# A fused attention and expert kernel on one core: a rotating fourth PSUM bank, no idle matmuls in the first steps, one more unit transposed by the crossbar, the last rows in three parts

## Chip, cores, metric

One core of a Trainium2 chip. The metric is the device time of one execution in microseconds (us). A program on one core has no other cores beside it to compare, so the state of a run is judged by its distance from the fastest run of the same kernel.

Differences in this study are tenths of a microsecond of some 475. For these the medians are too coarse. I therefore also use a second measure: the same ScalarE and VectorE instructions are paired in two traces, and the difference of their start times, from the start of each span, is read along the execution. It is called the **shift** below; negative is earlier than in the kernel before. Where no view of the profile shows a thing, it was read from the packed trace itself.

## The reference, cut

Attention over 4 batches, 8 heads, 768 rows of 64; queries and keys are assigned to one of 16 clusters, and only equal clusters see each other. The result, 3072 rows of 512, goes through four experts, weighted row by row.

```python
q_assign = argmax(q_n @ c_n.T); k_assign = argmax(k_n @ c_n.T)      # 16 clusters per head
mask = q_assign[:, :, :, None] == k_assign[:, :, None, :]
attn = softmax(where(mask, scale * q @ k.T, -1e9)); x = (attn @ v)   # -> 3072 x 512
p = domain_probs / (domain_probs.sum(-1, keepdims=True) + 1e-09)
for e in range(4):
    out += p[:, e:e + 1] * (maximum(x @ w1[e], 0) @ w2[e])           # 512 -> 1024 -> 512
```

## The kernel before

The mask is folded into the score product: 64 rows of a head's queries and keys are followed by 16 one-hot rows. Attention runs in steps of 512 scores, and the experts of earlier rows are woven between the steps so that TensorE always has work. A *unit* is 128 or 256 rows of the attention result.

PSUM has eight banks. Four of them matter here: three tagged `mo` and one tagged `misc`.

```python
PS_BUFS = {"s": 2, "av": 1, "av2": 1, "mo": 3, "misc": 1}
# ...
    ph = bank("mo")                    # expert, first layer:  eight matmuls of 256 columns
    po = bank("mo")[:, c]              # expert, second layer: eight matmuls of up to 512 columns
# ... scores of the cluster assignment of the next batch:
    put(at, lambda x=x, t=("mo", "misc")[z]: x.scores_split(t))
```

In the first steps an idle matmul stands ahead of the score matmuls. It writes zeros that the scores overwrite, and is there to hold TensorE's clock:

```python
WARM = range(4, 14)
# ... in attention(), one per step:
    if now in WARM:
        nc.tensor.matmul(sp[:, :256], blank[:, :128], blank[:, :256], start=True, stop=True)
    for x, (h, y) in enumerate(blocks[z:z + per] if b < ROWS else ()):
        nc.tensor.matmul(sp[:, x * n:(x + 1) * n], KF[...], QF[...], start=True, stop=True)
```

The one-hot rows of the keys of heads 6 and 7 come from other partitions, by four small transfers from SyncE's queue (`keep` copies to `oht`, `send` moves 16 x 384 elements of bf16, 12 KB):

```python
7: lambda: (k1.onehot(2), puts(k1, 0), k1.keep(), k1.send_all((2, 3))),
8: lambda: (qb.onehot_narrow(), qb.put_narrow(slice(0, 2), "dve")),
9: lambda: (puts(k1, 1), qb.put_narrow(slice(2, HG), "dve")),
```

The attention result is turned for the experts, by TensorE and a VectorE copy for the first four units, by the DMA crossbar for the rest:

```python
    if us[0] > 3:
        for m in range(nr):
            nc.sync.dma_start(out=xTs[us[0]][:, h2 // 2, m * 128:(m + 1) * 128],
                              in_=xn[:, m].rearrange("p j d -> p (j d)"), transpose=True)
        return
    due.setdefault(now + D_T + (us[0] > 1), []).append(turn)   # two TensorE transposes and dve()
```

The last 128 rows of the last expert are closed in two parts, so that the end is short:

```python
    end = (u, e, m) == (NU - 1, E - 1, len(rs) - 1)
    for c in (slice(0, DM // 2), slice(DM // 2, DM)) if end else (slice(0, DM),):
        po = bank("mo")[:, c]
        # eight matmuls, then oacc = po * p + oacc on VectorE
        if e == E - 1:
            nc.sync.dma_start(out=out[...], in_=oacc[:, c])
```

The softmax here doesn't subtract the row's maximum and nothing guards it: scores larger than these inputs give would overflow.

## Time and profile before

| | median | runs |
|---|---|---|
| time before | 476.23 us | 475.79 to 476.75 (4; the first three alone have the median 476.54) |
| span of the profiled execution | 473.6 us | |
| TensorE, busy share of the span | 98% | |
| all idle time of TensorE that the list of waits shows | 3.3 us in nine lines | |

In lines of a profile, PE is TensorE's matmuls, PEld its weight loads, DVE VectorE, ACT ScalarE, POOL GpSimd, and SPq the queue of transfers that SyncE issues; L728 is line 728 of the kernel. A row for a stretch of time gives its length, the busy us and the count of instructions of PE, PEld, DVE, ACT and POOL, then the granted clock, the busy share of the DMA engines and GB/s.

From the page of the kernel before: the span, and the two costliest groups of TensorE (source line, engine, operation, output and inputs, count; busy us, mean ns; idle time ahead of them):

```profile
span 473.6 us, 11333 instructions
...
L728 PE MATMUL ps_mo<-xT,w1b 128*128 128x256 bf16 (+1 forms) x1664 | 195.7, 264 | 0.0
...
L747 PE MATMUL ps_mo<-w2b,hT 128*128 128x512 bf16 (+1 forms) x725 | 186.2, 377 | 2.3
```

These are the two layers of the experts, in `mo` banks alone.

### The profile page before, as it was taken

Reading aid. Unit: us, or ns where it says so; the run is one execution under the profiler, and the core shown is the slowest. Engines: PE = TensorE matmul, PEld = TensorE weight load, DVE = VectorE, ACT = ScalarE, POOL = GpSimd, SP = SyncE. Lnnn points to the kernel's source line nnn. Section 1 sums busy time; section 2 is a strip of 40 time slices with the busy share of each in tenths; the row PEclk is TensorE's granted clock in tenths of the full one; section 3 lists DMA queues with packets and bytes.
Section 4 is the critical chain, followed back from the end, with each engine's and each line's share of the span. In section 5 each row is a group of like instructions: output and inputs, shape, how many; then the busy total and the mean of one; then the engine's idle time right before and its main releaser. Section 6 shows DMA issues by size and latency. Waiting matters only on the chain.

```text
span 473.6 us, 11333 instructions
## 1 busy us (share of the span) xinstructions
PE 464.2 (98%) x4488; PEld 333.2 (70%) x4539; DVE 227.1 (48%) x561; ACT 277.1 (59%) x502; POOL 187.8 (40%) x301
## 2 busy tenths in 40 slices
PE   8999999999999999999999999999999999999997
PEld 5778777777776767677676767776766766767665
DVE  5964764322315654322234544423878757665112
ACT  5767655454665556566555655665665685664342
POOL 5936469283353776370443942000332132221000
PEclk9999999999999999999999999999999999999999
DMA  8999962925564842603565657202100100100101
GB/s 279 259 211 345 240 123 35 173 44 164 98 126 108 197 104 41 154 21 60 154 141 122 118 113 160 68 20 70 51 12 8 53 11 8 35 29 12 44 2 45
DMA packets 74557, 48.01 MB, mean 101 GB/s; under 512 B 50248, under 2 KB 69256, under 8 KB 74504
## 3 DMA queue, kind: packets, MB, share of 16 engines
q1 hardware_dynamic: 65256, 37.96, 32.0%
q0 software_dynamic: 8576, 9.25, 11.0%
q8 instruction: 35, 0.57, 0.5%
q10 hardware_dynamic: 672, 0.08, 0.1%
q14 instruction: 18, 0.15, 0.1%
HBM read 37.31 MB, written 6.30 MB: 92 GB/s over the span
## 4 chain that ended last, share of the span: by engine, by line
PE 96%; DVE 1%; issue 1%; ACT 1%; ACTq 0%
PE ps_mo L728 35%; PE ps_mo L747 34%; PE ps_s L638 10%; PE ps_av L665 8%; PE ps_s L548 1%; PE ps_mo L242 1%; PE ps_misc L242 1%; PE ps_misc L548 1%; PE ps_s L87 1%; PE ps_mo L267 1%; PE ps_mo L400 1%; PE ps_misc L267 1%; PE ps_misc L400 1%; DVE oh L287 0%; DVE mx L284 0%
## 5 line engine op out<-in xcount | busy, mean ns | idle before, releaser
L644 ACT ACTIVATE at<-ps_s 128x512 bf16<-128x512 f32 x252 | 147.7, 595 | 118.3 <-PE ps_s L638 102.9
L728 PE MATMUL ps_mo<-xT,w1b 128*128 128x256 bf16 (+1 forms) x1664 | 195.7, 264 | 0.0
L747 PE MATMUL ps_mo<-w2b,hT 128*128 128x512 bf16 (+1 forms) x725 | 186.2, 377 | 2.3
L728 PEld LDWEIGHTS <-w1b 128*128 128x128 bf16 x1664 | 146.3, 98 | 25.0 <-issue 1.2
L734 ACT ACTIVATE hT<-ps_mo 128x512 bf16<-128x512 f32 x192 | 114.8, 598 | 60.9 <-PE ps_mo L728 58.0
L756 DVE SCALAR_TENSOR_TENSOR oacc<-ps_mo,psb,oacc 128x512 f32<-128x512 f32 (+1 forms) x73 | 54.1, 742 | 127.0 <-PE ps_mo L747 122.5
L747 PEld LDWEIGHTS <-hT 128*128 128x128 bf16 x776 | 67.0, 98 | 57.5 <-issue 3.1
L638 PE MATMUL ps_s<-qf,kf 80*128 80x256 bf16 (+1 forms) x456 | 82.8, 267 | 0.5 <-DMA kf<-oht 0.2
L665 PEld LDWEIGHTS <-at 128*128 128x128 bf16 x1152 | 69.9, 97 | 15.3 <-issue 1.7
L665 PE MATMUL ps_av<-vx,at 128*128 128x65 bf16 x1152 | 80.3, 193 | 0.2
L651 POOL TENSOR_TENSOR at<-at,same 128x512 bf16<-128x512 bf16 x24 | 28.3, 1177 | 96.6 <-ACT at L644 81.1
L638 PEld LDWEIGHTS <-kf 80*128 80x128 bf16 x456 | 42.5, 98 | 20.2 <-issue 1.3
L565 DVE TENSOR_SCALAR same<-qf,late 128x256 bf16<-128x256 bf16 x144 | 39.1, 324 | 0.0
L377 POOL COPY t<-t 128x768 uint16<-128x768 uint16 x32 | 36.3, 1143 | 0.0
L651 DVE TENSOR_TENSOR at<-at,same 128x512 bf16<-128x512 bf16 x48 | 21.6, 451 | 25.9 <-ACT at L644 25.8
L358 POOL COPY h<-raw 128x768 uint16<-128x768 uint16 x16 | 13.1, 829 | 36.0 <-DMA raw<-in_q_dram 29.7
L672 DVE RECIPROCAL zr<-ps_av 128x4 f32<-128x4 f32 (+1 forms) x50 | 8.9, 179 | 34.2 <-PE ps_av L665 34.1
L336 POOL DMA_DIRECT2D kf<-oht x32 | 15.5, 494 | 24.5 <-DMA oht<-oh 15.1
L361 POOL COPY h<-raw 128x768 uint16<-128x768 uint16 x16 | 13.5, 857 | 28.8 <-DMA raw<-in_q_dram 16.9
L754 DVE TENSOR_SCALAR oacc<-ps_mo,psb 128x512 f32<-128x512 f32 x18 | 13.5, 747 | 23.4 <-PE ps_mo L747 23.3
L416 POOL COPY st<-sct 128x384 uint16<-128x384 uint16 x16 | 10.7, 713 | 31.4 <-DMA sct<-scs 20.7
L336 POOL DMA_DIRECT2D qf<-oht x40 | 20.1, 510 | 4.5 <-DVE oht L313 3.9
(132 smaller groups left out, 288.4 us busy)
## 6 DMA issues: line engine op xcount, KB each, us to landing
raw<-in_v_dram SPq DMA_DIRECT2D x8, 768.0 KB, 6.6
out_dram<-oacc SPq DMA_DIRECT2D x23, 256.0 KB, 2.0
raw<-in_k_dram SPq DMA_DIRECT2D x7, 768.0 KB, 6.3
raw<-in_q_dram SPq DMA_DIRECT2D x6, 768.0 KB, 5.0
w1b<-in_moe_w_dram POOLq DMA_DIRECT2D x4, 1024.0 KB, 11.4
w2b<-in_moe_w_dram POOLq DMA_DIRECT2D x4, 1024.0 KB, 16.8
qf<-nos SPq DMA_DIRECT2D x2, 768.0 KB, 4.4
xT<-xn SPq DMA_TRANSPOSE x72, 2.4
```

The lines of the kernel that those rows point to most:

```text
L336: (nc.gpsimd if self.b or self.i0 and self.g else nc.sync).dma_start(out=self.rows(slice(D, D + CL), j, r), in_=self.oht[p0:p0 + CL, :self.w])
L361: pool(self.h16[:, z * HG * QW + c:z * HG * QW + c + 2 * QW], self.halves(raw[self.b, self.t, self.g])[:, 2 * c:2 * c + 4 * QW][:, z::2])
L377: pool(self.all[:, y * w:(y + 1) * w].bitcast(U16)[:, z::2], self.t16[:, (2 * z + y) * w:(2 * z + y + 1) * w])
L565: nc.vector.tensor_scalar(same[:, x * 256:(x + 1) * 256], clusters(b)[:, g, w, k // 2, k % 2, :], key_nos[b % 2][:, g, 8 * i + 4 * (k // 2 ...
L638: nc.tensor.matmul(sp[:, x * n:(x + 1) * n], KF[b % 2][:K, h, r, i * 128:(i + 1) * 128], QF[b % 2][:K, h, rs[0]:rs[-1] + 1, w * 128:(w + 1 ...
L644: nc.scalar.activation(at, sp, ACT.Exp, scale=scale)
L651: (nc.gpsimd if n4 in POOL_STEPS else nc.vector).tensor_tensor(at, at, same_cluster(b, w, cur), op=ALU.mult)
L665: nc.tensor.matmul(av[:, h % 2, m, :], at[:, c0:c0 + 128], VX[b % 2][:, h, 2 * i + r, :], start=(first and x == 0 and m == 0), stop=(last ...
L728: nc.tensor.matmul(ph[:, x * n:(x + 1) * n], W1[e][:, i, (f + x) * 128:(f + x + 1) * 128], xT[:, i, :], start=(i == 0), stop=(i == ND - 1))
L734: nc.scalar.activation(ht, ph, ACT.Relu)
L747: nc.tensor.matmul(po, hT[f // per][:, c0:c0 + 128], W2[e][:, f, c], start=(f == 0), stop=(f == NF - 1))
L756: nc.vector.scalar_tensor_tensor(oacc[:, c], po, pap, oacc[:, c], op0=ALU.mult, op1=ALU.add)
```

## The change

The intent: a fourth bank, free in the middle batches, joins the three that the experts use. The idle matmuls, which cost TensorE time, go. The fourth unit's eight transposes leave TensorE for the crossbar. The last rows close in three parts, the last half as long as before.

```diff
+    spare, turns = False, 0
+    def ring():
+        nonlocal turns
+        turns += 1
+        return bank("misc" if spare and turns % 4 == 0 else "mo")
@@ assignment scores
-            put(at, lambda x=x, t=("mo", "misc")[z]: x.scores_split(t))
+            put(at, x.scores_split)                  # takes ring() inside
@@ attention
-    WARM = range(4, 14)
-                    if now in WARM:
-                        nc.tensor.matmul(sp[:, :256], blank[:, :128], blank[:, :256],
-                                         start=True, stop=True)
-                            if us[0] > 3:
+                            if us[0] > 2:
@@ expert
-            ph = bank("mo")
+            ph = ring()
-            for c in (slice(0, DM // 2), slice(DM // 2, DM)) if end else (slice(0, DM),):
-                po = bank("mo")[:, c]
+            for c in (slice(0, 256), slice(256, 384), slice(384, DM)) if end else (slice(0, DM),):
+                po = ring()[:, c]
@@ woven
+                spare = PER_B + 4 <= step < PER_B * (B - 1)
```

More of the change, by code (lines that the diff above doesn't have):

```diff
@@ L390, in casts, with scores_split @@
             dve(late(self.t, self.b)[:, y:y + HG // 2], self.rows_of())
-        def scores_split(self, bank_tag):
-            sc = bank(bank_tag)
+        def scores_split(self):
+            sc = ring()
             for x in range(HG):
@@ L900, in woven @@
     def woven(works, upto):
+        nonlocal spare
         base, spent = step, 0.0
```

## The prediction

> **What bounds the kernel now.** I read the busy shares and the slices first, then the list of waits for TensorE alone, then busy time by stretches, then the groups, and last the timelines of the two ends.
>
> From the page of the kernel before (engines: busy us, share of the span, instructions; then tenths in 40 slices of 11.8 us):
>
> ```profile
> PE 464.2 (98%) x4488; PEld 333.2 (70%) x4539; DVE 227.1 (48%) x561; ACT 277.1 (59%) x502; POOL 187.8 (40%) x301
> PE   8999999999999999999999999999999999999997
> PEclk9999999999999999999999999999999999999999
> PE 96%; DVE 1%; issue 1%; ACT 1%; ACTq 0%
> ```
>
> TensorE is the bound from end to end: 98% busy, 96% of the chain that ended last. No other engine is over 59%. A busy share alone does not show that nothing is left, so I asked for waits. All idle time of TensorE over the span, by what ended it (us in total, times, longest):
>
> ```profile
> PE ps_s L87 <- DVE blank L80: 1.2, 1, 1.2
> PE ps_mo L276 <- ACT scs L271: 0.4, 1, 0.4
> PE ps_misc L296 <- DVE oh L287: 0.4, 2, 0.2
> PE ps_mo L296 <- DVE oh L287: 0.3, 1, 0.3
> PE ps_mo L267 <- DVE bdc L187: 0.2, 1, 0.2
> PE ps_s L638 <- DMA kf<-oht: 0.2, 1, 0.2
> PE ps_s L634 <- ACT at L644: 0.2, 1, 0.2
> ```
>
> No line has an expert matmul (L728, L747) waiting for its bank. The same query over 60 to 320 us, where the four banks will rotate, returns no wait at all. Busy time in two stretches of that part:
>
> ```profile
> 100.00:140.00 40.00, 39.74 (x385) 29.45 (x389) 11.92 (x21) 22.46 (x41) 19.22 (x45) 1.00 0.52 120
> 220.00:260.00 40.00, 39.79 (x378) 28.90 (x380) 12.40 (x24) 23.74 (x43) 14.39 (x17) 1.00 0.55 129
> ```
>
> The first pair after the length is TensorE: 39.7 of 40 us. Since ends of matmuls are modelled, I also took start-to-start distances from the trace: 109 ns for 256 columns, 216 ns for 512, 56 ns for 128, with a 90th percentile within 1 ns of the median. A distance of 432 ns occurs, but it is twice 216, and 725 of 768 second-layer matmuls are recorded, so those are lost records. Summed, what 60 to 320 us show above these distances is under 1 us, mostly around the small fp32 matmuls of L400.
>
> **What the Trainium skill says.** (1) "TensorE: Matmul & The Clock Gate", section "Wait — 56ns, not 53.3ns?": back-to-back distance is columns over 2.4 GHz plus some 2.5 ns, which gives 55.8, 109 and 216 ns. The trace agrees to 1 ns, so the middle is at the rate of the array. (2) "Perfetto Trace Analysis", its opening note: matmul busy time is a bad metric of what is left, as matmuls are pipelined. Hence the distances above. (3) The TensorE page, "What's actually happening": the clock halves after about one idle window of 3.4 us. That bears on taking idle matmuls out. The granted clock here is 1.00 in every stretch from 5.7 us on, also where the matmul stream fills only 0.65 (5.7 to 9.1) and 0.71 (9.1 to 12.5) of the time. (4) "DMA: Bandwidth & Descriptors", "Anatomy of one DMA": most of a transfer's fixed 2 us is waiting for the written bytes to be confirmed, not size. The trace agrees: the last output is issued at 470.86, its packets end at 472.3, the span at 473.6.
>
> **Part 1, four rotating banks.** Removes no instruction and adds none: the order listing has the same expert matmuls, with every fourth bank another one, and the score copies in the other bank. It can only shorten waits for banks on the path. There are none between 60 and 320 us. ScalarE and VectorE wait for TensorE there (58.0 us of ScalarE for L728, 122.5 us of VectorE for L747), so the readers of the banks are early, not late. Gain: 0.0, at most 0.2 us.
>
> **Part 2, ten idle matmuls less.** They are the group L634, ten of 256 columns between 15.6 and 22.9 us. On TensorE alone they are 10 x 0.109 = 1.09 us, and the chain of waits has them on it. But the path beside it is almost as long. SyncE and TensorE at that place:
>
> ```profile
> 19.36 2.50 SPq L336 DMA_DIRECT2D kf<-oht  x4
> ...
> 24.00 0.40 PE L638 MATMUL ps_s<-qf,kf 80*128 80x128 bf16 x4
> ...
> 26.09 0.33 PE L638 MATMUL ps_s<-qf,kf 80*128 80x128 bf16 x3 [0.18 <-DMA kf<-oht]
> ```
>
> The scores of heads 6 and 7 need four small transfers of one-hot rows. Their landings, from the semaphores in the trace, are 24.02, 24.60, 25.29 and 25.95 us, and the score matmuls that need them start at 24.23, 24.73, 25.43 and 26.09: each within 0.2 us of its landing. The transfers leave when VectorE has written their source (18.97 to 19.33), which follows a chain of transposes, maximum and comparison (16.03 to 18.31) that waits for VectorE twice. Of the ten matmuls only the first (15.58) stands ahead of that chain; two stand inside a wait for VectorE (idle 0.35 at 17.80), and the seven later ones stand beside the transfers. So of 1.09 us I expect 0.1 us to arrive: 0.11 of the first, and at most 0.2 us of slack at the landings. The rest becomes longer waits for these transfers. Clock: with the ten gone the stream still fills 0.69 of 15.9 to 19.3 and 0.75 of 19.3 to 22.7 (0.81 and 0.87 before), not below what kept full clock earlier.
>
> **Part 3, the fourth unit by the crossbar.** Group before (count, busy us, mean ns):
>
> ```profile
> L681 PE MATMUL ps_mo<-identb,xn 128*128 128x128 bf16 x24 | 3.7, 220 | 0.2 <-DVE xn L674 0.2
> ```
>
> Eight of these 24 go (71 to 111 us), with four VectorE copies. They stand in the dense part, so each is worth its distance: 8 x 0.056 = 0.45 us, all on the path. In exchange SyncE gets eight crossbar transposes of 1.2 us issue each. Is the data late then? Of the last head pair, VectorE is done at 105.7. SyncE's order puts it behind three transposes that end at 106.96; two issues more and 2.4 us to landing make about 110.5. The unit's first matmul (L728) starts at 117.73. Seven us of room: nothing comes back.
>
> **Part 4, the last rows in three parts.** The end of the kernel before:
>
> ```profile
> 470.16 1.03 SPq L759 DMA_DIRECT2D out_dram<-oacc  x2
> 470.35 0.48 DVE L756 SCALAR_TENSOR_TENSOR oacc<-ps_mo,psb,oacc 128x256 f32<-128x256 f32 x1 [0.39 <-PE ps_mo L747]
> ```
>
> TensorE: 8 x 0.109 = 0.87 becomes 16 x 0.056 = 0.89 us, +0.02. VectorE's last piece: 512 columns take 0.745 and 256 take 0.480 (both rows in the trace), so 1.035 ns a column and 128 fewer columns save 0.13 us. The piece before takes 0.35 us and ends before the last matmul (0.45 us later). The last transfer halves to 64 KB: of its 2.7 us only the packets' part shrinks (estimate 0.05 to 0.1 us, from 8 packets per engine at 46 ns). Sum: -0.2 us.
>
> **Sum.** 0.0 - 0.1 - 0.45 - 0.2 = -0.75 us: 476.54 becomes 475.8 us.
>
> **The rivals.** (a) All ten idle matmuls count, because the transfers land earlier than now once they are issued earlier. Then -1.09 in place of -0.1: 474.8. For it: L634 is on the chain. Against: the landings decide 24.2 to 26.1, and the queues are full there (DMA share over 1.0 in every stretch from 3 to 33 us). (b) Removed idle matmuls cost the clock: one or two windows of 3.4 us at half rate, so +2 to +4 us: 478 to 480. Against: the shares above. I give it 4%. (c) The rotation does pay, through bank waits that the records hide: a few ns at each of some 190 evictions, 0.5 to 1 us. Against: the median distances equal the array's rate. (d) The crossbar transposes hold up SyncE's in-order queue, and input loads behind them (109 us) start 2.4 us later. GpSimd waits for those loads, but their results are used 25 us later: no change expected.
>
> **Range and chances.** The runs of the kernel before span 1.0 us (475.79 to 476.75), as large as the effect. Half of (a) gives 475.3; everything failing but part 3 gives 476.1. With the scatter of a median (about 0.4 us) I take 474.9 to 476.6. A change over 2% means 9.5 us. Nothing here reaches that: all idle time of TensorE listed above is under 3 us. So within 2% has 0.99.
>
> **What will show it.** Part 1: TensorE's idle list over 60 to 320 us is empty in both, and the busy time by stretches is equal. Part 2: L634 gone, granted clock still 1.00, and the idle time of TensorE (or of its weight loads, which the profile calls issue) between 15 and 27 us up by about 1 us, with the first unit's expert matmuls (28.8 us before) starting only 0.1 us earlier. If they start a full us earlier, rival (a) is right. Part 3: L681 x16, and the distance between a point at 65 and one at 120 us shorter by 0.45 us. Part 4: from the last matmul to the end of the span 0.2 us less. I am wrong by more than the range if the clock falls after 15 us, or if middle stretches shorten by more than 0.5 us beyond part 3.

## The result

Ratios here are the mean time of one kernel's fast runs over that of the other's of the same rounds, so they are not quite the ratio of the medians quoted beside them.

| | before | after |
|---|---|---|
| median (runs) | 476.23 (475.79 to 476.75, 4) | 475.87 (475.32 to 476.10, 4) |
| profiled span | 473.60 | 473.54 |

The ratio is 0.999, 95% interval 0.9973 to 1.0008: **the same**. The prediction said 475.8 in a range of 474.9 to 476.6. The page of the kernel after, same parts as shown of the kernel before:

```profile
span 473.5 us, 11380 instructions
...
PE 466.0 (98%) x4529; PEld 332.2 (70%) x4529; DVE 226.9 (48%) x558; ACT 277.2 (59%) x502; POOL 187.5 (40%) x301
...
PEclk9999999999999999999999999999999999999999
...
PE 95%; DVE 2%; DMA 1%; issue 0%; ACT 0%; SPq 0%; ACTq 0%
```

TensorE went up in busy time (464.2 to 466.0) with less work. That is no slowdown: x4529 equals the weight loads' x4529, while before 4488 of 4539 were recorded. No record of a matmul is lost this time. The clock row is full throughout.

The list of waits of TensorE over the whole span (us in total, times, longest; the first six of eight lines):

```profile
PE ps_s L95 <- DVE blank L88: 1.2, 1, 1.2
PE ps_misc L304 <- DVE oh L295: 0.6, 2, 0.4
PE ps_s L642 <- ACT at L648: 0.4, 2, 0.3
PE ps_mo L284 <- ACT scs L279: 0.4, 1, 0.4
PE ps_mo L304 <- DVE oh L295: 0.4, 1, 0.4
PE ps_s L642 <- DMA kf<-oht: 0.4, 2, 0.2
```

Line numbers are 4 to 8 higher than before at these places. All of these lie at the start. Three have grown most: the wait for `oh` in `misc` (0.4 to 0.6), for ScalarE's `at` (0.2 to 0.4) and for the transfers `kf<-oht` (0.2 to 0.4). Between 60 and 320 us the list is empty, as it was. The same two stretches of the middle (TensorE's busy us first):

```profile
100.00:140.00 40.00, 40.00 (x390) 29.54 (x389) 11.41 (x20) 22.79 (x40) 19.87 (x45) 1.00 0.58 126
220.00:260.00 40.00, 40.00 (x383) 28.89 (x380) 12.49 (x25) 24.08 (x44) 14.02 (x16) 1.00 0.62 128
```

40.00 of 40, where the kernel before showed 39.7 and 39.8. Those 0.2 to 0.3 us were lost records and no room to win, as the prediction held from the distance of 432 ns.

The shift shows where time came and went, after minus before:

| at (us) | shift (us) | what lies there |
|---|---|---|
| 13 | +0.23 | first inputs landed later (differs between runs of one code, see below) |
| 22 | -0.31 | idle matmuls gone |
| 25 | +0.11 | the scores of heads 6 and 7 wait for the four transfers |
| 73.5, 83, 95, 111 | 0.00, -0.11, -0.23, -0.34 | two TensorE transposes less at each |
| 111 to 463 | -0.34 | constant: nothing from the rotation |
| end of span | -0.06 | 0.28 lost in the last 10 us (0.21 by the table below, which counts from the start of a last matmul that is 0.05 shorter; 0.02 is TensorE's) |

In this pair of profiles, then, three parts did what was predicted, and the **tail** (all that follows the last matmuls) did not. The records of the two tails (last matmul's start; VectorE's last piece; issue and landing of the last output; end of SyncE's list of closing waits; end of span; all in us from the span's start):

| kernel | last matmul | VectorE done | issue | landing | list done | span | last matmul to end |
|---|---|---|---|---|---|---|---|
| before | 470.04 | 470.83 | 470.86 | 472.68 | 472.72 | 473.60 | 3.56 |
| after | 469.77 | 470.38 | 470.57 | 472.19 | 472.66 | 473.54 | 3.77 |

VectorE finishes 0.61 us after the start of the last matmul instead of 0.79: the predicted 0.13 is there, and 0.05 more because the last matmul is itself shorter. But the issue follows 0.19 us later, not 0.03, because SyncE is still issuing the second part (until 470.48). And after the landing comes something that the prediction had no term for. The program ends with nine waits of SyncE, each for two semaphores, in a fixed order; together they cover every semaphore of a transfer. One such wait takes some 62 ns when its semaphores are already there. Transfers from SyncE and ScalarE take eight semaphores in rotation (100, 101, 105 to 110, then 100 again), and the closing list goes through them in the same order. Before, the last output fell on semaphore 110, which is last in that order: one wait is left after its landing. The change adds nine transfers (eight transposes, which leave the rotation of eight where it was, and one output part, which moves it by one). Now the last output falls on semaphore 100, the second pair in the order, and eight waits are left: 472.19 to 472.66. The output landed 0.49 us earlier and the span ended 0.06 us earlier. Behind the list the engines still wait for one another; that takes 0.88 us in both kernels.

The timelines of both engines at the end of the kernel after (start, duration, engine, line, operation, idle time before):

```profile
468.26 2.12 DVE L760 SCALAR_TENSOR_TENSOR oacc<-ps_mo,psb,oacc 128x512 f32<-128x512 f32 x4 [4.47 <-PE ps_mo L751]
```

```profile
469.04 1.94 SPq L763 DMA_DIRECT2D out_dram<-oacc  x4
```

The rows before and the last three pieces are drawn together. VectorE ends at 470.38, SyncE's issues run on to 470.98: what VectorE gave early, SyncE's queue passed on late.

### The profile page after: what moved, and what is told of

Its sections match the earlier page's. It is cut to its first block, busy times and chain, and to the rows that moved or that the text cites. A ratio compares the mean times of both kernels' runs of the same rounds, so it can differ in the third digit from the quotient of the medians.

```text
span 473.5 us, 11380 instructions
## 1 busy us (share of the span) xinstructions
PE 466.0 (98%) x4529; PEld 332.2 (70%) x4529; DVE 226.9 (48%) x558; ACT 277.2 (59%) x502; POOL 187.5 (40%) x301
## 4 chain that ended last, share of the span: by engine, by line
PE 95%; DVE 2%; DMA 1%; issue 0%; ACT 0%; SPq 0%; ACTq 0%
PE ps_mo L732 31%; PE ps_mo L751 30%; PE ps_s L642 9%; PE ps_av L669 7%; PE ps_misc L751 5%; PE ps_misc L732 4%; PE ps_s L555 1%; PE ps_mo L250 1%; DMA kf<-oht 1%; PE ps_mo L408 1%; PE ps_misc L250 1%; PE ps_misc L555 1%; PE ps_s L95 1%; DVE kf L323 1%; PE ps_mo L275 0%; PE ps_misc L275 0%
## 5 line engine op out<-in xcount | busy, mean ns | idle before, releaser
L732 PE MATMUL ps_mo<-xT,w1b 128*128 128x256 bf16 (+1 forms) x1464 | 172.8, 264 | 0.0
L751 PE MATMUL ps_mo<-w2b,hT 128*128 128x512 bf16 (+2 forms) x680 | 165.5, 374 | 0.0
L738 ACT ACTIVATE hT<-ps_mo 128x512 bf16<-128x512 f32 x168 | 100.4, 598 | 57.9 <-PE ps_mo L732 56.3
L760 DVE SCALAR_TENSOR_TENSOR oacc<-ps_mo,psb,oacc 128x512 f32<-128x512 f32 (+2 forms) x63 | 46.1, 732 | 118.4 <-PE ps_mo L751 118.2
L751 PE MATMUL ps_misc<-w2b,hT 128*128 128x512 bf16 x104 | 26.5, 379 | 0.0
L732 PE MATMUL ps_misc<-xT,w1b 128*128 128x256 bf16 (+1 forms) x200 | 26.2, 268 | 0.0
```

The source lines that it names most:

```text
L732: nc.tensor.matmul(ph[:, x * n:(x + 1) * n], W1[e][:, i, (f + x) * 128:(f + x + 1) * 128], xT[:, i, :], start=(i == 0), stop=(i == ND - 1))
L738: nc.scalar.activation(ht, ph, ACT.Relu)
L751: nc.tensor.matmul(po, hT[f // per][:, c0:c0 + 128], W2[e][:, f, c], start=(f == 0), stop=(f == NF - 1))
L760: nc.vector.scalar_tensor_tensor(oacc[:, c], po, pap, oacc[:, c], op0=ALU.mult, op1=ALU.add)
```

## The experiments

Twelve kernels, each correct. Chip 7 unless noted; the kernel before had the median 476.19 to 476.22 in its runs there, 475.59 on chip 14. The last column is the change of shift in the part of the execution where the edit works.

| label | median (runs) | ratio to before, 95% | in the profile |
|---|---|---|---|
| a_rotation | 476.11 (5) | 0.9999 (0.9987 to 1.0011) | 0.0 |
| a_no_idle | 475.79 (5) | 0.9994 (0.9983 to 1.0006) | +0.05 |
| a_crossbar | 475.83 (5) | 0.9985 (0.9972 to 0.9998) | -0.45 |
| a_tail3 | 476.52 (6) | 1.0012 (1.0001 to 1.0023) | tail +0.45 |
| e_tail2 | 474.94 (4) | 0.9975 (0.9960 to 0.9989) | tail 3.45 |
| e_sem | 475.15 (4) | 0.9979 (0.9966 to 0.9992) | tail 3.33 |
| e_idle2 | 476.50 (4) | 1.0006 (0.9993 to 1.0019) | +0.67 |
| e_bank2 | 487.24 (6) | 1.0232 (1.0219 to 1.0244) | +12.2 in all |
| e_put (chip 14) | 476.19 (5) | 1.0010 (0.9997 to 1.0024) | +0.49 |
| e_put_idle (chip 14) | 476.50 (5) | 1.0024 (1.0011 to 1.0036) | +0.79 |
| best (chip 14) | 480.40 (4) | 1.0098 (1.0084 to 1.0113) | +6.2 |
| best2 | 474.99 (4) | 0.9972 (0.9958 to 0.9987) | tail 3.14 |

The competing theories: mine is that part 1 is worth nothing, part 2 almost nothing as the transfers wait beside it, part 3 its full 0.45, and that the tail loses to the closing waits. The rivals: the rotation pays in hidden bank waits; the idle matmuls count in full, or hold the clock; the tail's loss is noise or SyncE's queue.

**Scatter first.** Profiles of kernels whose start or middle is the same code still differ in four places: the first inputs (-0.2 to +0.7 us at 13 us), and around 171 and 283 us, where a small fp32 score matmul waits for a GpSimd merge (0 to 0.9), and from 24 to 28 us, where four small transfers land 4.5 to 5.2 us after their issue. A jump at these places is not laid to an edit below.

### One part at a time

**Rotation alone** (the kernel before with `ring()` and `spare`, nothing else).

> The kernel before with only the four rotating banks. My theory (no wait for a bank is on the path between 60 and 320 us): the same, 0.0 us, at most 0.2 us faster; the same ScalarE and VectorE instructions start within 0.05 us of the kernel before all through 60 to 430 us. Rival (a few ns are hidden at each eviction): starts drift earlier steadily through 75 to 310 us, by 0.5 to 1 us in all.

The shift is +0.03 from 75 to 153 us and +0.11 after a jump at 171: no drift over 250 us in which the four banks rotate. A few ns at each of some 190 evictions would have shown as a slope of 0.5 to 1 us. Part 1 is worth 0.0.

**Idle matmuls gone, alone.**

```diff
-    WARM = range(4, 14)
+    WARM = ()
```

> The kernel before with only the ten idle matmuls taken out. My theory (the four small transfers of one-hot rows and the VectorE chain ahead of them are the path there): about 0.1 us faster from 26 us on, the idle time of TensorE between 15 and 27 us up by about 0.9 us, granted clock 1.00. Rival 1 (they are on TensorE's path): 1.1 us faster from 26 us on. Rival 2 (they held the clock): granted clock under 1.00 after 15 us and 2 to 4 us slower.

The shift goes +0.09 to -0.51 at 23.7 us, then back to +0.14. The waits of TensorE from 15 to 27 us:

```profile
PE ps_s L638 <- DMA kf<-oht: 0.4, 1, 0.4
PE ps_misc L296 <- DVE oh L287: 0.4, 1, 0.4
PE ps_s L638 <- ACT at L644: 0.3, 1, 0.3
```

and where the lead is lost, in TensorE's timeline:

```profile
24.67 0.42 PE L638 MATMUL ps_s<-qf,kf 80*128 80x128 bf16 x4 [0.41 <-DMA kf<-oht]
```

The bracket says: idle 0.41 us, ended by the landing of `kf<-oht`. The same instruction started at 24.47 before. The four transfers tell why:

| issue to landing (us) | 1 | 2 | 3 | 4 |
|---|---|---|---|---|
| before | 19.36 to 24.02 | 20.02 to 24.60 | 20.64 to 25.29 | 21.28 to 25.95 |
| a_no_idle | 19.35 to 24.54 | 20.01 to 24.74 | 20.63 to 25.32 | 21.27 to 26.03 |

The first inputs came 0.09 us later in this profile, so counted from them the transfers left 0.10 us earlier, as predicted for the first of the ten matmuls. The last landed 0.08 us later all the same. The first scores that need each transfer start 0.13, 0.13, 0.13 and 0.14 us after its landing; before, it was 0.45, 0.13, 0.14 and 0.14. So three of the four landings held TensorE up already, and now all four do. This refutes rival (a) of the prediction, for which the transfers had to leave, and land, a full us earlier. The granted clock stayed 1.00, which refutes rival (b).

**Idle matmuls doubled.**

```diff
-                        nc.tensor.matmul(sp[:, :256], blank[:, :128], blank[:, :256],
-                                         start=True, stop=True)
+                        for _ in range(2):
+                            nc.tensor.matmul(sp[:, :256], blank[:, :128], blank[:, :256],
+                                             start=True, stop=True)
```

> The kernel before with twenty idle matmuls in place of ten, two at each of the same steps. If the path beside them is only just as long as TensorE's own, adding is not hidden as removing was: theory 0.5 to 0.9 us slower from 26 us on, with TensorE's idle time between 15 and 27 us going to nearly nothing. If there is wide slack beside them: 0.0 to 0.1 us slower. If each counts on the path: 1.1 us slower.

The shift grows from -0.01 to +0.66, so 0.67 of the added 10 x 0.109 = 1.09 us arrive. Stretch 15 to 27 us in the kernels before, after and this one:

```profile
15.00:27.00 12.00, 11.26 (x165) 9.32 (x162) 10.37 (x35) 8.87 (x16) 10.03 (x18) 1.00 1.18 223
```

```profile
15.00:27.00 12.00, 10.76 (x157) 8.61 (x154) 10.41 (x35) 8.78 (x16) 10.04 (x18) 1.00 1.18 223
```

```profile
15.00:27.00 12.00, 11.87 (x170) 9.95 (x165) 10.12 (x33) 8.65 (x16) 9.98 (x18) 1.00 1.17 226
```

TensorE is busy 11.26, 10.76 and 11.87 of 12 us at the same granted clock (1.00, third from the end). Doubling the filler used up the slack and put TensorE itself on the path; removing it left slack that nothing could use. The kernel before stands close to the border between the two: the filler costs 0.0 to 0.1, and as much again costs 0.7.

**The transfers taken away**, to see what the idle matmuls are worth without them. VectorE writes the rows of heads 6 and 7 straight from PSUM. `e_put` has no idle matmuls, `e_put_idle` has them.

```diff
-        7: lambda: (k1.onehot(2), puts(k1, 0), k1.keep(), k1.send_all((2, 3))),
+        7: lambda: (k1.onehot(2), puts(k1, 0)),
-        9: lambda: (puts(k1, 1), qb.put_narrow(slice(2, HG), "dve")),
+        9: lambda: (puts(k1, 1), qb.put_narrow(slice(2, HG), "dve"), puts(k1, 2), puts(k1, 3)),
```

> The kernel before without the ten idle matmuls, and without the four small transfers: VectorE writes the one-hot rows of heads 6 and 7 in place, two steps later, as it does for the other heads. My theory (the transfers are the wall at 24 to 26 us): with them gone the removed idle matmuls come through, and from 26 us on the kernel is earlier than without idle matmuls alone, by 0.2 to 0.7 us, until the next wait. Rival (VectorE is the wall, not the transfers): as without idle matmuls alone or up to 1 us slower, as VectorE gets 1.2 us more.

> The same with the ten idle matmuls kept. If the transfers were what hid the removal, the difference between this and the one without idle matmuls is well over 0.1 us: 0.3 to 0.9 us. If VectorE's own chain hides it, the difference stays 0.1 to 0.2 us.

This separates less than I hoped, and the expectation for `e_put` was missed: it is not 0.2 to 0.7 us earlier than `a_no_idle` from 26 us on but 0.44 later, as its rival said. Both got later: `e_put` by 0.49 (+0.40 to +0.89), `e_put_idle` by 0.79 (-0.10 to +0.69), probably because VectorE, now with more to do, became the next wall (its first normalised rows `xn` come 1.36 us later in `e_put`). The idle matmuls are worth 0.30 us between the two, more than the 0.0 to 0.1 with the transfers in place, which fits a hidden cost that comes into view when the transfers go. But it is one difference of two profiles beside a new wall, and I do not call it shown.

**Crossbar for the fourth unit, alone.**

```diff
-                            if us[0] > 3:
+                            if us[0] > 2:
```

> The kernel before with only the fourth unit's transposes on the crossbar. My theory: 0.45 us faster, in four steps of 0.11 us between 71 and 111 us, and nothing given back at 117 us; the last transfer still lands on the last semaphore in SyncE's closing list (eight transfers more leave the rotation of eight semaphores where it was), so the whole 0.45 us reaches the end. Rival (SyncE's in-order queue holds up loads behind it): the gain is partly gone by 220 us.

The group of TensorE transposes that are left:

```profile
L681 PE MATMUL ps_mo<-identb,xn 128*128 128x128 bf16 x16 | 2.6, 221 | 0.1
```

24 became 16, and the shift falls from +0.56 to +0.11 in four steps of 0.11 us: twice 0.056 for each head pair. That is -0.45, to 0.01 us what the distances said. In the kernel after, the data is ready long before it is used. SyncE's and TensorE's timelines there:

```profile
106.95 2.46 SPq L694 DMA_TRANSPOSE xT<-xn  x2
```

```profile
117.39 0.60 PE L732 MATMUL ps_mo<-xT,w1b 128*128 128x256 bf16 x4
```

The last two transposes are issued by 109.4, the second lands at 110.53, 2.33 us after its issue began, and the unit's first matmul is at 117.39: the predicted seven us of room. The issue of a load, at 108.94 before, comes at 111.86, and nothing later shows it (rival (d)).

**Three parts at the end, alone.**

```diff
-            for c in (slice(0, DM // 2), slice(DM // 2, DM)) if end else (slice(0, DM),):
+            for c in (slice(0, 256), slice(256, 384), slice(384, DM)) if end else (slice(0, DM),):
```

> The kernel before with only the last rows in three parts. Theory formed from the trace of the changed kernel: the last transfer lands 0.15 us earlier relative to the last matmuls, but one transfer more moves it to the first of the eight rotating semaphores, which SyncE's closing list waits for second, so that eight more closing waits of 0.06 us each come after the landing (some 0.45 us) where there was none: the span is 0.25 to 0.3 us longer. Rival (as predicted: only the sizes count): 0.2 us shorter.

The whole run is slower than before, if by little (1.0012, interval above 1). Part of it is this profile's scatter at 171 us:

```profile
PEld ps_misc L400 <- POOL t L377: 1.0, 2, 0.8
```

But the tail is counted from the last matmul and has none of that: 4.00 us against 3.56. The last output lands on semaphore 100, eight closing waits follow and take 0.47 us. The tail grew by more than the expected 0.25 to 0.3: the landing, which should have come 0.15 us earlier after the last matmul, came 0.02 later, as SyncE's issue of the second part ended only at 472.63 and the last issue began at 472.72.

### What ends the tail

`e_tail2` is the kernel after with two parts again. `e_sem` keeps three parts, but sends an earlier output, that of the rows of unit NU-2, by GpSimd's queue, which is outside the rotation of eight; this moves the last transfer by one place.

```diff
 # e_sem
-                    nc.sync.dma_start(
+                    (nc.gpsimd if (u, m) == (NU - 2, 0) else nc.sync).dma_start(
```

> The changed kernel with the last rows in two parts again, everything else as changed. Closing-list theory: the last transfer is back on the last semaphore of SyncE's closing list, so landing to end of the span falls from about 1.3 us back to about 0.9, and the kernel is about 0.3 us faster than the changed one, 0.55 us faster than before. Rival (the third part pays): 0.2 us slower than the changed kernel.

> The changed kernel, three parts kept, but one output of the unit before the last is issued from GpSimd, on another set of semaphores, so that the last transfer falls on the last semaphore of SyncE's closing list. Nothing else about the last rows changes. Closing-list theory: 0.4 us faster than the changed kernel, 0.75 us faster than before; closing waits after the last landing: one instead of eight. Rival (the time after the landing is fixed, whatever the semaphore): as the changed kernel.

| kernel | parts | last matmul to issue | issue to landing | semaphore | waits after | landing to list done | last matmul to end |
|---|---|---|---|---|---|---|---|
| before | 2 | 0.82 | 1.82 | 110 | 1 | 0.04 | 3.56 |
| e_tail2 | 2 | 0.83 | 1.69 | 110 | 1 | 0.05 | 3.45 |
| after | 3 | 0.80 | 1.62 | 100 | 8 | 0.47 | 3.77 |
| a_tail3 | 3 | 0.96 | 1.69 | 100 | 8 | 0.47 | 4.00 |
| e_sem | 3 | 0.81 | 1.61 | 110 | 1 | 0.05 | 3.33 |
| best2 | 3 | 0.64 | 1.58 | 110 | 1 | 0.05 | 3.14 |

`e_sem` is the clean pair to the kernel after: the same three parts, the same 0.81 and 1.61 us to landing, and 0.05 in place of 0.47 us behind it. Its SyncE timeline is that of the kernel after, only 0.7 us later:

```profile
469.75 1.95 SPq L763 DMA_DIRECT2D out_dram<-oacc  x4
```

The transfer costs the same, and what comes after it does not. By time the two are not told apart: `e_sem` is 0.7 us faster by medians of other rounds, and the intervals of their ratios to the kernel before overlap. Against the kernel before, `e_tail2` was expected 0.55 us faster and `e_sem` 0.75; they are 1.2 and 1.0 by the ratios, more than their records explain. So what shows the cause is the records of the tails, not the times. The size of the cost follows the count of waits: the two kernels of the `e_put` pair have four transfers fewer on SyncE's queue. The rotation then puts their last output on semaphore 106, four places before 110, and so it was, with five waits after landing. Four more waits at 62 ns make 0.25 us. Measured from landing to the end of the list, they take 0.29 us, where one wait takes 0.04 to 0.05. Their tails, two parts, are 3.72 and 3.75, where the seven two-part kernels with one wait have 3.44 to 3.73, mean 3.55. As two-part tails of equal code scatter by 0.3 us, single differences of 0.1 in the other columns are not to be read. For the same reason it is not shown that the third part pays at all: `e_sem` with three parts and `e_tail2` with two have the same time within noise.

### Fewer banks

If three banks suffice with nothing to spare, two should hurt.

```diff
-    PS_BUFS = {"s": 2, "av": 1, "av2": 1, "mo": 3, "misc": 1}
+    PS_BUFS = {"s": 2, "av": 1, "av2": 1, "mo": 2, "misc": 1}
```

> The kernel before with two banks for the experts in place of three (no fourth anywhere). If three are well more than enough in the middle, two should show where waits begin: the reader of a bank takes 0.6 to 0.75 us, a group of matmuls 0.9 to 1.7 us, so the bank is free in time unless ScalarE is held by an exponential: theory 0.5 to 5 us slower in all, with TensorE waits for ScalarE (L734) appearing in 60 to 320 us. If banks were near the limit (rival: rotation should have paid): over 10 us slower.

The only run that leaves the 2%: +5.9 us by 117 us, +8.07 at 310, +12.2 at the end. My size for the whole was missed, and the total is the rival's, that bank waits are near. But by place it is not where the fourth bank rotates: of the 12.2 us the middle, 117 to 310, has 2.2 and the last batch 4. TensorE's waits from 60 to 330 us, an empty list with three banks (the first four of seven lines):

```profile
PE ps_mo L400 <- DVE oacc L756: 1.0, 2, 0.5
PE ps_mo L276 <- DVE oacc L754: 0.6, 1, 0.6
PE ps_mo L747 <- DVE oacc L756: 0.6, 1, 0.6
PE ps_mo L747 <- ACT hT L734: 0.5, 2, 0.2
```

This is how a bank wait looks: `ps_mo` waits for the engine that empties `ps_mo`. It shows in the list when it is there, though not in full: the seven lines make 3.5 us, and the shift grows by some 6 us over the same stretch. So the empty list of the other kernels is evidence, and the flat shift of `a_rotation` is the stronger one. Two banks are too few, three are enough, and the fourth has nothing left to remove.

### Towards a better kernel

`best` takes the kernel after, `e_sem`, the last output from ScalarE's queue (idle there, so it need not wait for SyncE's second issue), and the crossbar for one unit more.

```diff
-                    nc.sync.dma_start(
+                    (nc.gpsimd if (u, m) == (NU - 2, 0) else
+                     nc.scalar if end and c.stop == DM else nc.sync).dma_start(
-                            if us[0] > 2:
+                            if us[0] > 1:
```

> The changed kernel with the closing list mended (one earlier output from GpSimd), the last transfer issued from ScalarE's queue, which is idle then, and the third unit's transposes on the crossbar too. Theory: 0.4 us from the closing list, 0.1 us from not waiting for SyncE to issue, 0.45 us from eight more transposes off TensorE if their data come in time: 0.9 us faster than the changed kernel, 1.3 us faster than before. Rival: the third unit's rows are late because SyncE waits for input loads at 47 to 60 us, and TensorE waits: up to 3 us slower.

The tail is 3.15, but the kernel is 1% slower, 4.8 us by the medians, more than its rival's 3. Up to 62 us the shift falls from -0.07 to -0.50: the third unit's transposes do pay their 0.43. Then it jumps to +6.56. TensorE's longest wait, new, in its timeline:

```profile
67.87 0.40 PE L732 MATMUL ps_mo<-xT,w1b 128*128 128x256 bf16 x1 [3.95 <-DMA xT<-xn]
```

ahead of it SyncE's queue, and the stretches around it:

```profile
60.38 2.46 SPq L694 DMA_TRANSPOSE xT<-xn  x2
```

```profile
60.00:64.00 4.00, 3.92 (x41) 2.90 (x39) 2.50 (x5) 2.28 (x4) 0.00 (x0) 1.00 1.29 178
64.00:67.00 3.00, 0.00 (x0) 0.00 (x0) 0.15 (x1) 0.00 (x0) 1.04 (x3) 1.00 1.30 109
67.00:74.00 7.00, 6.13 (x35) 4.98 (x36) 2.28 (x5) 1.79 (x3) 6.91 (x15) 0.51 0.39 118
```

SyncE's queue is not what holds them up. VectorE has written the last rows at 59.87, and the third unit's last two transposes are issued at 60.38 and 61.61. But they land at 67.59 and 67.82, 7.2 and 6.2 us after their issue, where the fourth unit's last two took 2.3 in the kernel after. The DMA engines are full here (share 1.24 from 60 to 68 us). In the kernel after, the same transposes landed in 2.3 us where the share was 0.17 (67 to 71.5 us) or 0.35 (107 to 110.5), in 3.8 where it was 0.54 (79 to 83), and in 7.1 where it was 0.96 (80 to 87.5). With 2.3 us the data would have come at about 63.9, about when TensorE needed it (an estimate). One unit on, there were seven us of room; here it is short by four.

The wait is a little more than half of the jump. The rest is the clock: after these 4.0 us without a matmul the granted clock is 0.50 for 6.8 us (67.04 to 73.87), and six us of work at half the clock take 3.0 us longer. All four runs have it: their mean clock is 0.993 or 0.996, and the two with 0.993 are 1.2 to 1.6 us slower than the other two. So rival (b) of the prediction was wrong for these idle matmuls, not for this kernel: their removal left TensorE's matmuls no wait over 0.4 us from 15 to 27 us, and a wait ten times as long cost the clock. The 0.45 us that a unit's transposes cost are a fair price there.

`best2` is the same without that last step (`us[0] > 2` stays).

> The changed kernel with only the end mended: one output of the unit before the last from GpSimd, so that the last transfer falls on the last semaphore of SyncE's closing list, and that last transfer issued from ScalarE's queue, which is idle. The third unit stays off the crossbar. Closing-list theory, from the profiles so far: from the start of the last matmul to the end of the span 3.15 to 3.2 us, as in the kernel with both mends and the third unit on the crossbar, against 3.77 in the changed kernel; so 0.6 us faster than the changed kernel, 1.0 us (0.7 to 1.3) faster than before. Rival (the end is noise): as the changed kernel, 0.4 us faster than before.

474.99 us, 0.9972 of before (0.9958 to 0.9987), 1.2 us by the medians and 1.3 by the ratio: more than the expected 1.0, at the upper end of 0.7 to 1.3. The issue comes 0.03 us after VectorE is done instead of 0.19, as it does not queue behind SyncE's second issue. It beats the kernel before, if by less than 2%; `e_tail2` (474.94) and `e_sem` (475.15) do too, and the three can't be told apart by time. Against the kernel after (475.87, other rounds) it is 0.9 us by medians.

## Why the prediction was right, and which step was not

The time was right, with one of the four terms wrong in sign. That the two errors in it, of the start and of the gain, cancelled to within 0.1 us is luck.

- **Part 1, 0.0.** Right. No slope in the shift (`a_rotation`), and a list that does show bank waits when there are any (`e_bank2`). The waits of ScalarE and VectorE that were quoted for the middle, 58.0 and 122.5 us, are those of the whole span; in 60 to 320 us they are 14.6 and 84.3.
- **Part 2, -0.1.** Right within what can be read. From 13 to 28 us the shift changes by -0.12 in the kernel after, +0.05 in `a_no_idle`, -0.01 in `e_tail2`, -0.03 in `e_sem`, -0.02 in `best` and +0.23 in `best2` (where the fourth transfer took 5.08 us), so 0.0 in the mean; kernels that kept the ten have -0.05 to +0.07. The removed time came back as waits for `oh`, `at` and the transfers, at the landings that were named. One of the four start times was read wrongly: no score matmul starts at 24.23, and the first that needs the first transfer started at 24.47, 0.45 us after the landing. The other three landings set the time, so nothing came of it. Rivals (a) and (b) fell with the issue times and the clock.
- **Part 3, -0.45.** Right to 0.01, in four steps. The row with the mean of 220 ns would have said 1.8 us for eight; the distance of 56 ns was the right price.
- **Part 4, -0.2.** Failed: the step that took all 2.7 us from the last issue to the end of the span for the transfer's, fixed but for its packets. In the kernel before they are 1.82 us to the landing, 0.04 of the closing list and 0.88 in which the engines wait for one another. (The packets end at 472.33, and the landing follows 0.35 us later.) The list grows when the last output falls on an early semaphore, and the sum had no term for it. Measured, VectorE and the shorter last matmul gave 0.18, of which SyncE's serial issue kept 0.16, another step without a term. Issue to landing gave 0.20, and the closing waits took 0.43: together +0.21. The packets' share was set too low: 1024 bytes take 46 ns and 512 bytes 27, so eight of them 0.15 us less (an estimate); from issue to landing, seven two-part kernels with one wait have 1.69 to 1.99, mean 1.81, and the three that send a third part from SyncE 1.61 to 1.69, mean 1.64.
- **Sum.** In this pair of profiles the shift has -0.12, -0.45 and +0.28, together -0.29, and the span's -0.06 less the +0.23 of the first inputs is the same. Predicted was -0.75, and the medians of four runs each have -0.36. The predicted 475.8 rests on a first median of 476.54; four runs of the same kernel have 476.23. That start was 0.3 too high and the gain 0.4 too large, so the end came out within 0.1. The change is worth nearer 0.3 than 0.75 us by the profiles; by time neither value, nor zero, is excluded, for the interval of the ratio reaches from -1.3 to +0.4 us.

Two more slips had no effect: the second layer has 776 matmuls and not 768, and the idle list of TensorE has nine lines and 3.3 us, of which seven are shown.

Still open: how long a landing takes at the end without scatter, and what the idle matmuls cost with the transfers gone and VectorE not in the way.

## What to carry to other kernels

On a saturated engine, work taken out pays only where nothing runs beside it: price it by start-to-start distance, then look for the transfer that was being waited for anyway. A resource added (a bank) is worth what the list of waits says, and an experiment with one fewer shows whether the list can be believed. When the last microsecond is cut, count on to the very end of the program: one more transfer moved the last landing near the front of the closing list and took back twice what a shorter last part had been expected to save. When a change makes TensorE wait, look at the granted clock as well: in `best` a wait of 4.0 us cost 3.0 more.

## What the Trainium skill lacked or had wrong

- No page has it: this program ends with nine waits for pairs of semaphores in a fixed order, 0.06 us each. Where in the rotation of eight the last transfer falls decides whether 0.05 or 0.47 us follow its landing (`e_sem` against the kernel after).
- "DMA: Bandwidth & Descriptors", "Anatomy of one DMA": the section is about transfers issued from GpSimd, and gives some 2 us fixed plus bytes over 436 GB/s, so an estimate of 2.15 us for 64 KB. Those here were issued from SyncE: 64 KB in 1.61 and 1.62 us from issue to landing at the quiet end, 12 KB in 4.6 to 5.2 us among the first loads (DMA share over 1.1). It has the fixed part constant; here the same kind of transfer, a 128 x 128 transpose, landed in 2.3 us where the DMA share was 0.17 to 0.35, in 7.1 where it was 0.96 and in 6.2 to 7.2 where it was 1.24.
- "Advanced Engine Details and Errata", "X-Bar Transpose (TRN2)": it calls transposes as fast as regular transfers. It gives no time for their issue: here two 128 x 128 transposes hold SyncE's queue for 2.46 us, one 768 KB load for 0.56 us.
- "TensorE: Matmul & The Clock Gate": it speaks of idle and busy windows of 3.4 us, not of how full a window must be. Here the clock stayed at 1.00 with TensorE busy 10.76 of 12 us by the profile, and where the matmul stream, by the prediction's count, fills 0.65 of a window. For a whole window without a matmul the page is borne out: after 4.0 us idle the clock was 0.50 for 6.8 us (`best`).
